# Channel attention and gated unit in seven-product blocks: the sums of GpSimd moved to VectorE and to accumulating DMAs, and two more of eight pairs in eight products

## The chip, the core and the metric

The kernel runs on one core of one Trainium2 chip. The core has five engines that run side by side, each through its own queue in order: TensorE (PE, with PEld for its weight loads), VectorE (DVE), ScalarE (ACT), GpSimd (POOL) and SyncE (SP, which here only issues DMAs). The metric is the device time of one execution in microseconds.

## The reference, cut to what matters

```python
qn = q / (norm(q, axis=1) + 1e-6);  kn = k / (norm(k, axis=1) + 1e-6)    # over the 6080 tokens
s  = kn.transpose(0, 2, 1) @ qn / tau                                     # 4 batches of 256x256
a  = softmax(s, axis=-1);  y = v @ a                                      # y: 4 x 6080 x 256
h  = y.reshape(24320, 256) @ w_in                                         # 256 -> 2048
out = (h * sigmoid(1.702 * h)) @ w_out                                    # 2048 -> 256
```

All inputs are float32; the two weights come as float64 and are narrowed on the chip.

## The kernel before, in words

**Work.** For each batch the scores are summed over 25 units of up to two rows of 128 tokens (`Attention.unit`), and beside them the sums of squares of q and k for the norms. The softmax gives `a`, and `weights` folds it into the first weight, so that h is v times one matrix. The 6080 tokens of a batch are cut into six chunks of 1024 (the last of 960). The 2048 features are cut into eight pairs of blocks of 2x128. So the main loop has 4 x 6 x 8 = 192 places, one pair at a place; `front` makes h and its gates for it, `back` the share of the output.

**Products.** A product is three matmuls of 128x128 by 128x512, since each float32 operand is split into a high and a low part in float32r (a cast on ScalarE makes the high part, a subtraction on VectorE, `low`, the other). `front` makes the four blocks of h in seven products (M1 to M7) of sums of blocks of v (`values`) and of the weights. `back` does the second multiplication, by G, the gated blocks, in one of two ways. In a pair of the first kind ("S") it forms four sums of gated blocks, P1 to P4, and makes seven products; in a pair of the second kind ("N") it needs no sums and makes eight. `GROUPS` says how many pairs of each kind stand in each half of a chunk: three S and one N. The first chunk of batch 0 has N pairs alone.

**Buffers.** Tiles live in named slots, and the next tile in a slot waits for every user of the one before. Sums of an S pair: `gp` (one slot) and, in place, `ga` (two). Split parts: `gi` and `gj` (two each), `gr` (three, `NR`). Second weights: `wo` (two). At the end of each half chunk one PSUM bank, K, is used four times in a row: it is read out as `ka`, `kb`, `kc` and `kd`; the last takes the products of N pairs, whose `gj` and `wo` are held until then.

**Who sums.** P1, P2 and P4 are made by VectorE, P3 by GpSimd (line 868). The four sums of v of a chunk are GpSimd's (`eng="POOL"`, line 705). The squares of batch 0 are added half by VectorE, half by GpSimd; those of batches 1 to 3 by GpSimd alone (lines 489 to 499). Batches 0 and 1 load q and k four rows at a time into the slots `gr` and `gj`, before the main loop needs these; for batch 1 the squares go through the slot `gp`, one tile at a time, and run beside the first chunk.

**Order.** The program is not written in its final order. Each instruction is a node with an engine, an estimated cost, dependencies and a due time; `Plan.order` plays the engines against each other, gives a free engine the ready node with the earliest due time, and the resulting sequence is issued. A load's landing is estimated as 50 ns + 2.6 ns per KB, plus a `lag` (line 261). Once issued, each engine keeps its sequence: an instruction that waits holds all behind it on its engine.

Of the kernel before, what the change touches and what calls it, by code (L numbers as in the profile page):

```python
# [11 lines left out]
F32 = mybir.dt.float32  # L12
F32R = mybir.dt.float32r
U32 = mybir.dt.uint32
AF = mybir.ActivationFunctionType
ALU = mybir.AluOpType
# [4 lines left out]
P = 128  # L21
# [4 lines left out]
HW = CH // 2  # L26
# [153 lines left out]
    return 350 + 2.0 * n  # L180


GROUPS = ((3, 1), (3, 1))
FIRST = ((0, 4), (0, 4))
NV = 8
NR = 3
GLAG = 12.0


# [1 line left out]
def channel_attention_then_glu(  # L191
# [10 lines left out]
    nc = tc.nc  # L202
# [9 lines left out]
    RT = 4  # L212
# [8 lines left out]
    g = Plan()  # L221

    def sbuf(slot, shape, dtype=F32, name=None):
        return g.buf(slot, lambda: sb.tile(list(shape), dtype, tag=slot, name=name or slot))
# [31 lines left out]
    def plain(ap):  # L256
        return ap.bitcast(F32) if ap.dtype == F32R else ap

    def load(dst, src, kb, deps=(), uses=(), due=0.0):
        return g.add(  # L260
            "SP", 50 + kb * 2.6, lambda: nc.sync.dma_start(plain(dst()), plain(src())), deps, uses, due, lag=2200,
        )

    def load_cast(dst, src, kb, deps=(), uses=(), due=0.0):
# [156 lines left out]
    class Attention:  # L421
# [39 lines left out]
        def unit(self, u, due, after=()):  # L461
            t0, nt, pp = self.units[u]
            if t0 not in self.raw:
                t = sbuf(f"ra{u % 2}", [P, 2, UT, C], F32, "raw")
                view = (lambda i: t()[:, i, :nt, :]) if pp == P else (lambda i: t()[:pp, i, 0, :])
                ns = [
                    load(
                        lambda i=i: view(i), lambda i=i: self.rows(i, t0, nt, pp), 128 * nt, after, [t], due - 8,
                    )
                    for i in range(2)  # L470
                ]
                for o in range(nt):
                    self.raw[t0 + o] = (t, o, ns)
            buf, o, _ = self.raw[t0]
            ready = [n for j in range(nt) for n in self.raw[t0 + j][2]]
            w = 2 * nt * C
            src = lambda: buf()[:pp, :, o : o + nt, :]
            acc = self.acc
            if u == 0:
                self.acc_n = [g.add(  # L480
                    "ACT", act(w), lambda: nc.scalar.activation(acc(), src(), AF.Square), ready, [buf, acc], due + 0.5,
                )]
            else:
                sq = sbuf("gp" if self.b == 1 else "sq", [P, 2, UT, C], F32, "sq")
                s = g.add(
                    "ACT", act(w),
                    lambda: nc.scalar.activation(sq()[:pp, :, :nt, :], src(), AF.Square), ready, [buf, sq], due + 1,  # L487
                )
                if self.b == 0:
                    parts = [("DVE", slice(0, 1)), ("POOL", slice(1, 2))]  # L490
                else:
                    parts = [("POOL", slice(0, 2))]
                new = []
                for e, (eng, sl) in enumerate(parts):
                    a = lambda sl=sl: acc()[:pp, sl, :nt, :]
                    new.append(tt(
                        a, a, lambda sl=sl: sq()[:pp, sl, :nt, :], ALU.add, w // len(parts),
                        [s, self.acc_n[min(e, len(self.acc_n) - 1)]], [sq, acc], due + 1.5, eng,
                    ))
                self.acc_n = new  # L500
            if self.direct:
                op, ok, uses = buf, ready, [buf]
            else:
                hl = sbuf("hl", [P, 2, UT, 2, C], F32R, "hl")
                hs = [
                    load_cast(
                        lambda i=i: hl()[:, i, :nt, 0, :] if pp == P else hl()[:pp, i, 0, 0, :],
                        lambda i=i: self.rows(i, t0, nt, pp), 128 * nt, after, [hl], due - 6,
                    )
                    for i in range(2)  # L510
                ]
                l = low(
                    lambda: hl()[:pp, :, :nt, 1, :], src, lambda: hl()[:pp, :, :nt, 0, :], w,
                    hs + ready, [buf, hl], due,
                )
                ok, uses = [l], [hl]
            S = self.S if self.direct else bank("Z", "s")
            news = []
            for j in range(nt):
                first = j == 0 and (u == 0 or not self.direct)  # L520

                def fn(j=j, first=first):
                    for i in range(NC2):
                        ci = slice(i * P, (i + 1) * P)
                        out = S()[:, i * C : (i + 1) * C]
                        begin = first and i == 0
                        if self.direct:
                            nc.tensor.matmul(
                                out, lhsT=buf()[:pp, 1, o + j, ci], rhs=buf()[:pp, 0, o + j, :],
                                start=begin, stop=True, skip_group_check=True,  # L530
                            )
                            continue
                        for m, (l, r) in enumerate(((0, 0), (0, 1), (1, 0))):
                            nc.tensor.matmul(
                                out, lhsT=hl()[:pp, 1, j, l, ci], rhs=hl()[:pp, 0, j, r, :],
                                start=begin and m == 0, stop=True, skip_group_check=True,
                            )

                n = g.add(
                    "PE", 864 if self.direct else 720, fn, ok + [self.first] + news[:1], [*uses, S], due + 2 + 0.1 * j,  # L540
                )
                if first and self.direct:
                    self.first = n
                news.append(n)
            if self.direct:
                self.last += news
            else:
                total = self.S
                self.last = [
                    g.add("DVE", dve(HW), lambda: nc.vector.tensor_copy(total(), S()), news, [S, total], due + 2.5)  # L550
                    if u == 0 else
                    tt(
                        lambda: total(), lambda: S(), lambda: total(), ALU.add, HW, news + self.last, [S, total],
                        due + 2.5,
                    )
                ]
# [145 lines left out]
    vslot = [0]  # L702
    ORDER = (M1, M2, M6, M5, M7, M3, M4)

    def values(b, c, due, after=(), eng="POOL"):
        o, w = chunks[c]
        hw = w // 2
        raw = sbuf("vr", [P, NC2, CH], F32, "v_raw")
# [107 lines left out]
    def back(ck, u, fr, wo, wb, t):  # L816
# [50 lines left out]
                    product(acc, a(i), src, j, ok, at)  # L867
                at += 0.7
        else:
            gp = sbuf("gp", [P, 2, HW], F32, "gp")  # L870
            gr = sbuf(f"gr{rcount[0] % NR}", [P, 2, 2, HW], F32R, "gr")
            rcount[0] += 1
            p1 = tt(lambda: gp()[:, 0, :hw], blk(0), blk(1), ALU.add, hw, [g11, g12], [ga, gp], t + 8.2)
            p3 = tt(blk(0), blk(0), blk(3), ALU.add, hw, [p1, g22], [ga], t + 8.8, "POOL")
            p2 = tt(lambda: gp()[:, 1, :hw], lambda: gp()[:, 0, :hw], blk(3), ALU.add, hw, [p1, g22], [ga, gp], t + 9.4)
            p4 = tt(blk(2), blk(2), lambda: gp()[:, 1, :hw], ALU.add, hw, [p2, g21, lo], [ga, gp], t + 12)
            hr = cast(lambda: gr()[:, 0, :, :hw], lambda: gp()[:, :, :hw], 2 * hw, [p1, p2], [gp, gr], t + 15)
            lr = low(
                lambda: gr()[:, 1, :, :hw], lambda: gp()[:, :, :hw], lambda: gr()[:, 0, :, :hw], 2 * hw,
                [hr], [gp, gr], t + 16,  # L880
            )
            pair = lambda: ga()[:, 0:3:2, :hw]
            hj = cast(lambda: gj()[:, 0, :, :hw], pair, 2 * hw, [p3, p4], [ga, gj], t + 13)
            lj = low(
                lambda: gj()[:, 1, :, :hw], pair, lambda: gj()[:, 0, :, :hw], 2 * hw, [hj], [ga, gj], t + 14,
            )
            a = lambda i: (lambda m: wt()[:, m, i, :])
            ck.k1.append(product(K, a(M1), gi, 0, lo, t + 13))
# [90 lines left out]

    def fetch_wo(ck, u, due, after=()):  # L980
        woslot[0] += 1
        w = sbuf(f"wo{woslot[0] % 2}", [P, 2, NI, P], F32R, "wo")
        cut = slice(1, 1 + NI) if ck.kinds[u][2] else slice(0, 4)
        n = load(
            lambda: w()[:, :, : cut.stop - cut.start], lambda: wout_d[u, :, :, cut, :], 640,
            [wout_ready[u], *after], [w], due,
        )
        return w, n
# [18 lines left out]
    keep_warm(8, (), -9e8, "X")  # L1007
    EARLY = -400.0
    t0, slot = 0, 0
    stage = ["gr0", "gj0", "gr1", "gj1", "gr2"]  # L1010
    sizes = [UT] + [RT] * ((T + 1 - UT + RT - 1) // RT)
    tau_n = None
    for r, room in enumerate(sizes):
# [21 lines left out]
    nxt = Attention(1)  # L1035
    t0, slot = 0, 0
    while t0 < T:
        nxt.load_direct(t0, RT, f"gr{slot % 3}", -80.0 + 2.2 * t0)
        t0 += RT
        slot += 1  # L1040
    for u in range(nu):
# [96 lines left out]
```

## Time and profile before

| | |
|---|---|
| median of 3 runs | 2467.65 us (2467.39 to 2470.84) |
| profiled execution | 2472.11 us, of it 2470.3 us from first to last instruction |
| PE busy | 2207.9 us (89%) |
| DVE busy | 1943.2 us (79%) |
| ACT busy | 1647.6 us (67%) |
| POOL busy | 700.1 us (28%) |
| mean granted TensorE clock | 0.971 of full |

An engine's busy time counts its instructions from start to end, with whatever slows them down; idle time is told by what ended it. Of PE, a busy stretch is not a stretch at full rate: matmuls overlap, and the clock that was granted has two levels.

### The profile page before, as it was taken

How to read it: one execution, taken by the hardware profiler on the slowest of the kernel's cores; microseconds unless marked ns; L12 is line 12 of the kernel's file. 1: busy time of each engine (PE TensorE's matmuls, PEld its weight loads, DVE VectorE, ACT ScalarE, POOL GpSimd, SP SyncE). 2: the span in 40 equal slices, each digit the busy share in tenths (PEclk: the TensorE clock that was granted, in tenths of full speed). 3: DMA queues.
4: the chain of work that ended last, by engine and by line, in shares of the span. 5: the costliest groups of instructions: out<-in, count | busy, mean ns of one | idle time of the engine just before them, and what ended most of it. 6: DMA issues, size and time to landing. Idle time of an engine off the chain costs nothing.

```text
span 2470.3 us, 27428 instructions
## 1 busy us (share of the span) xinstructions
PE 2207.9 (89%) x9694; PEld 1762.4 (71%) x9694; DVE 1943.2 (79%) x2167; ACT 1647.6 (67%) x2355; POOL 700.1 (28%) x440
## 2 busy tenths in 40 slices
PE   8588899989988899989898899989999999999998
PEld 7466677767776677767677677767777777777777
DVE  5888877778778787877887877878787777877776
ACT  4466776766656667766576666767777777777775
POOL 4442212334333331213333343322122122212211
PEclk9699999999999999999999999999999999999999
DMA  8676666566565654866566656656765555545553
GB/s 283 209 257 245 235 255 233 186 221 226 190 222 184 226 179 159 285 236 202 194 212 218 223 176 212 204 188 224 253 215 194 179 192 196 192 159 202 190 181 137
DMA packets 206872, 517.19 MB, mean 209 GB/s; under 512 B 16272, under 2 KB 84880, under 8 KB 205712
## 3 DMA queue, kind: packets, MB, share of 16 engines
q1 hardware_dynamic: 180816, 490.53, 56.6%
q0 software_dynamic: 25920, 24.91, 4.3%
q8 instruction: 77, 1.26, 0.2%
q14 instruction: 59, 0.48, 0.1%
HBM read 448.53 MB, written 66.85 MB: 209 GB/s over the span
## 4 chain that ended last, share of the span: by engine, by line
PE 42%; DVE 26%; DMA 16%; ACT 8%; issue 4%; POOL 3%; SPq 0%; DVEq 0%; POOLq 0%; ACTq 0%
PE ps_o L764 11%; PE ps_k L764 8%; PE ps_X L764 8%; PE ps_Y L764 6%; PE ps_Z L764 5%; DMA wo<-wout_d 5%; DVE ga L276 4%; DVE gi L291 3%; DMA hl<-in_k 3%; DVE gp L276 3%; ACT ga L790 3%; DMA raw<-in_k 3%; DVE gj L291 2%; DVE hl L291 2%; DVE v L291 2%
## 5 line engine op out<-in xcount | busy, mean ns | idle before, releaser
L275 POOL TENSOR_TENSOR ga<-ga 128x512 f32<-128x512 f32 (+1 forms) x138 | 229.6, 1664 | 1044.0 <-DVE gp L276 1016.2
L764 PE MATMUL ps_X<-v,w 128*128 128x512 f32 (+1 forms) x1728 | 498.2, 397 | 17.0 <-ACT ps_Z L268 16.6
L790 ACT ACTIVATE ga<-ga 128x512 f32<-128x512 f32 (+1 forms) x384 | 235.6, 626 | 258.1 <-DVE ga L276 256.6
L764 PE MATMUL ps_o<-gi,wo 128*128 128x512 f32 (+1 forms) x1476 | 401.3, 394 | 1.9 <-DVE gi L291 1.3
L291 DVE TENSOR_TENSOR gi<-ga,gi 128x1536 fp32r<-128x1536 f32 (+2 forms) x192 | 344.7, 1796 | 68.2 <-ACT gi L268 67.9
L764 PEld LDWEIGHTS ps_X<-v,w 128*128 128x128 f32 x1728 | 322.4, 191 | 99.8 <-ACT ps_Z L268 37.7
L764 PE MATMUL ps_Y<-v,w 128*128 128x512 f32 (+1 forms) x1152 | 337.9, 402 | 45.5 <-DVE ga L276 37.0
L764 PE MATMUL ps_Z<-v,w 128*128 128x512 f32 (+1 forms) x1152 | 333.3, 397 | 27.4 <-DVE ss L276 12.4
L764 PE MATMUL ps_o<-gj,wo 128*128 128x512 f32 (+1 forms) x1152 | 316.6, 396 | 28.6 <-DVE oc L276 8.0
L275 POOL TENSOR_TENSOR acc<-acc,sq 128x1024 f32<-128x1024 f32 (+2 forms) x96 | 216.6, 2257 | 389.9 <-ACT sq L487 389.8
L764 PEld LDWEIGHTS ps_o<-gi,wo 128*128 128x128 f32 x1476 | 281.5, 191 | 61.8 <-DVE gi L291 2.8
L764 PEld LDWEIGHTS ps_Y<-v,w 128*128 128x128 f32 x1152 | 212.8, 192 | 111.2 <-DVE ga L276 53.3
L764 PEld LDWEIGHTS ps_Z<-v,w 128*128 128x128 f32 x1152 | 216.5, 191 | 86.8 <-DVE ss L276 18.8
L764 PEld LDWEIGHTS ps_o<-gj,wo 128*128 128x128 f32 x1152 | 214.9, 190 | 83.5 <-DVE gj L291 11.0
L268 ACT CAST gi<-ga 128x1536 fp32r<-128x1536 f32 (+2 forms) x192 | 258.5, 1346 | 5.1
L276 DVE TENSOR_TENSOR ga<-ps_Y,m 128x512 f32<-128x512 f32 (+1 forms) x192 | 130.4, 679 | 153.0 <-PE ps_Y L764 96.7
L764 PE MATMUL ps_k<-gr,wb 128*128 128x512 f32 (+1 forms) x828 | 217.4, 390 | 3.4 <-ACT kb L268 1.3
L291 DVE TENSOR_TENSOR gj<-ga,gj 128x1024 fp32r<-128x1024 f32 (+1 forms) x138 | 192.6, 1396 | 21.6 <-ACT gj L268 20.3
L268 ACT CAST gj<-ga 128x1024 fp32r<-128x1024 f32 (+1 forms) x138 | 143.9, 1043 | 76.4 <-DVE ga L276 70.1
L764 PE MATMUL ps_k<-gi,wo 128*128 128x512 f32 (+1 forms) x414 | 133.0, 424 | 69.0 <-DMA wo<-wout_d 45.7
L291 DVE TENSOR_TENSOR gr<-gp,gr 128x1024 fp32r<-128x1024 f32 (+1 forms) x138 | 185.0, 1340 | 5.6 <-ACT gr L268 5.4
L268 ACT CAST gr<-gp 128x1024 fp32r<-128x1024 f32 (+1 forms) x138 | 143.5, 1040 | 58.5 <-DVE gp L276 47.7
(120 smaller groups left out, 3269.7 us busy)
## 6 DMA issues: line engine op xcount, KB each, us to landing
w<-w_d SPq DMA_DIRECT2D x184, 896.0 KB, 4.7
wo<-wout_d SPq DMA_DIRECT2D x138, 640.0 KB, 5.5
wb<-wout_d SPq DMA_DIRECT2D x138, 256.0 KB, 3.8
wo<-wout_d SPq DMA_DIRECT2D x54, 512.0 KB, 4.9
w_d<-wst SPq DMA_DIRECT2D x24, 896.0 KB, 5.1
v_raw<-in_vT SPq DMA_DIRECT2D x20, 1024.0 KB, 8.8
out_T<-oc SPq DMA_DIRECT2D x80, 256.0 KB, 5.4
wi<-win_d SPq DMA_DIRECT2D x32, 512.0 KB, 5.6
```

The costliest lines, as they stand in the source:

```text
L268: return g.add("ACT", act(n, psum), lambda: nc.scalar.copy(dst(), src()), deps, uses, due)
L275: return g.add("POOL", pool(n), lambda: nc.gpsimd.tensor_tensor(dst(), a(), b(), op=op), deps, uses, due)
L276: return g.add("DVE", dve(n), lambda: nc.vector.tensor_tensor(dst(), a(), b(), op=op), deps, uses, due)
L291: lambda: nc.vector.tensor_tensor(dst(), src(), hi().bitcast(F32), op=ALU.subtract),
L764: nc.tensor.matmul(dst, lhsT=l(a), rhs=r(b), start=begin and n == 0, stop=True, skip_group_check=True,)
L790: lambda: nc.scalar.activation(dst(), src(), AF.Gelu_apprx_sigmoid, scale=sign), deps, uses, at,
```

## The change

1. **GROUPS**: two S and two N pairs in each half of a chunk in place of three and one. With the first chunk as it was, 92 of the 192 places are S pairs and 100 are N pairs (138 and 54 before).
2. **P1 and P3** of an S pair are one VectorE operation of 2x512 elements, which reads one block twice (`broadcast_to`). P1 to P4 all stand in `gp`, now four blocks; nothing is written into `ga` any more.
3. **The sums of v** are VectorE's.
4. **The squares of batches 1 to 3** are added by DMAs that accumulate into `acc`, issued by GpSimd. Batch 0 is as it was.
5. **Slots and estimates**: two slots of `gr` in place of three, three of `wo` in place of two; the loads of batches 0 and 1 go through one `gr` slot less; a load's lag is 3000 ns in place of 2200.

```diff
-GROUPS = ((3, 1), (3, 1))
+GROUPS = ((2, 2), (2, 2))
-NR = 3
+NR = 2
+NWO = 3
@@ load
-... deps, uses, due, lag=2200,
+... deps, uses, due, lag=3000,
@@ Attention.unit
-                if self.b == 0:
-                    parts = [("DVE", slice(0, 1)), ("POOL", slice(1, 2))]
-                else:
-                    parts = [("POOL", slice(0, 2))]
+                parts = [("DVE", slice(0, 1)), ("POOL", slice(1, 2))] if self.b == 0 else [("DMA", slice(0, 2))]
...
+                    if eng == "DMA":
+                        new.append(g.add(
+                            "POOL", 1200, lambda a=a, more=more: nc.gpsimd.dma_start(a(), more(), accum_op=ALU.add),
+                            deps, [sq, acc], due + 1.5, lag=3500,
+                        ))
@@ values
-    def values(b, c, due, after=(), eng="POOL"):
+    def values(b, c, due, after=(), eng="DVE"):
@@ back, a pair of the first kind
-            gp = sbuf("gp", [P, 2, HW], F32, "gp")
+            gp = sbuf("gp", [P, 4, HW], F32, "gp")
-            p1 = tt(lambda: gp()[:, 0, :hw], blk(0), blk(1), ALU.add, hw, [g11, g12], [ga, gp], t + 8.2)
-            p3 = tt(blk(0), blk(0), blk(3), ALU.add, hw, [p1, g22], [ga], t + 8.8, "POOL")
-            p2 = tt(lambda: gp()[:, 1, :hw], lambda: gp()[:, 0, :hw], blk(3), ALU.add, hw, [p1, g22], [ga, gp], t + 9.4)
-            p4 = tt(blk(2), blk(2), lambda: gp()[:, 1, :hw], ALU.add, hw, [p2, g21, lo], [ga, gp], t + 12)
+            p13 = tt(
+                lambda: gp()[:, 0:3:2, :hw], lambda: ga()[:, 0:1, :hw].broadcast_to([P, 2, hw]),
+                lambda: ga()[:, 1:4:2, :hw], ALU.add, 2 * hw, [g11, g12, g22], [ga, gp], t + 8.2,
+            )
+            p2 = tt(lambda: gp()[:, 1, :hw], lambda: gp()[:, 0, :hw], blk(3), ALU.add, hw, [p13], [ga, gp], t + 9.4)
+            p4 = tt(lambda: gp()[:, 3, :hw], blk(2), lambda: gp()[:, 1, :hw], ALU.add, hw, [p2, g21], [ga, gp], t + 12)
...
@@ fetch_wo, loads of batches 0 and 1
-        w = sbuf(f"wo{woslot[0] % 2}", [P, 2, NI, P], F32R, "wo")
+        w = sbuf(f"wo{woslot[0] % NWO}", [P, 2, NI, P], F32R, "wo")
-    stage = ["gr0", "gj0", "gr1", "gj1", "gr2"]
+    stage = ["gr0", "gj0", "gr1", "gj1"]
-        nxt.load_direct(t0, RT, f"gr{slot % 3}", -80.0 + 2.2 * t0)
+        nxt.load_direct(t0, RT, f"gr{slot % 2}", -80.0 + 2.2 * t0)
```

In the orders below the numbers tell tiles of one name apart. VectorE at one S pair of the last batch, before: P1, P2 and P4, and the low parts of `gr` and `gj` (P3 is GpSimd's).

```order
L276 TENSOR_TENSOR gp_12905<-ga_12832 128x512
L276 TENSOR_TENSOR gp_12905<-gp_12905,ga_12832 128x512
L276 TENSOR_TENSOR ga_12832<-ga_12832,gp_12905 128x512
L291 TENSOR_TENSOR gr_12924<-gp_12905,gr_12924 128x1024
L291 TENSOR_TENSOR gj_12931<-ga_12832,gj_12931 128x1024
```

The same place now:

```order
L277 TENSOR_TENSOR gp_14672<-ga_14646 128x2x512
L277 TENSOR_TENSOR gp_14672<-gp_14672,ga_14646 128x512
L277 TENSOR_TENSOR gp_14672<-ga_14646,gp_14672 128x512
L292 TENSOR_TENSOR gi_14677<-ga_14646,gi_14677 128x1536
L292 TENSOR_TENSOR gr_14697<-gp_14672,gr_14697 128x1024
```

The first operation is twice as wide and no operation of GpSimd stands between it and `gj`.

GpSimd in the last batch before, with the sums of v (`v_t`, `v_raw`) between the P3 of six pairs:

```order
L275 TENSOR_TENSOR v_t_14793<-v_raw_14744 128x512
L275 TENSOR_TENSOR ga_14736<-ga_14736 128x512
L275 TENSOR_TENSOR v_t_14793<-v_t_14793,v_raw_14744 128x512
L275 TENSOR_TENSOR v_raw_14744<-v_raw_14744 128x512
L275 TENSOR_TENSOR ga_14913<-ga_14913 128x512
```

VectorE at such a place now:

```order
L277 TENSOR_TENSOR ga_15117<-ps_X_15063,m5_15089 128x512
L277 TENSOR_TENSOR v_t_15150<-v_raw_15099 128x512
L277 TENSOR_TENSOR v_t_15150<-v_t_15150,v_raw_15099 128x512
L277 TENSOR_TENSOR v_raw_15099<-v_raw_15099 128x512
L283 SCALAR_TENSOR_TENSOR gj_15157<-ga_15117,gj_15157 128x1024
L292 TENSOR_TENSOR gi_15174<-ga_15117,gi_15174 128x1024
```

Three of the four sums of v stand in VectorE's queue behind the load of `v_raw` and ahead of a pair's low parts; GpSimd's queue has no sums there any more.

ScalarE in the first chunk before, at the end of batch 1's squares (`sq`), in front of the sixth pair (`m5` begins a pair):

```order
L487 ACTIVATE sq_1295<-raw4_1063 128x2x256
L268 COPY m5_1314<-ps_Z_1305 128x512
L268 CAST cw_1320<-cv_1271 128x512
L268 COPY ps_Z_1305<-ps_X_1310 128x512
L487 ACTIVATE sq_1330<-raw4_1063 64x2x256
L268 COPY ps_Y_1344<-ps_X_1310 128x512
```

The same squares now, one or two pairs further on:

```order
L269 COPY m5_1495<-ps_Z_1485 128x512
L269 COPY ps_Z_1485<-ps_X_1490 128x512
L269 CAST cs_1502<-cf_1466 128x1024
L269 COPY ps_Y_1512<-ps_X_1490 128x512
L488 ACTIVATE sq_1515<-raw4_1359 128x2x256
L793 ACTIVATE ga_1520<-ps_Z_1485 128x512
L793 ACTIVATE ga_1520<-ga_1520 128x512 x2
L852 ACTIVATE gj_1547<-ga_1520 128x1024
L269 COPY wf_1549<-ps_w_1527 128x512
L793 ACTIVATE ga_1520<-ps_Y_1512 128x512
L269 CAST gi_1555<-ga_1520 128x1024
L488 ACTIVATE sq_1562<-raw4_1359 64x2x256
```

The last square of batch 1 now stands in the seventh pair of the first chunk. Each square waits until the DMA that adds the one before it has landed, and what stands behind it on ScalarE waits with it.

## Rows read from the trace of the kernel before

**Rows 1.** The page: engines, and the granted TensorE clock in 40 slices.
```profile
PE 2207.9 (89%) x9694; PEld 1762.4 (71%) x9694; DVE 1943.2 (79%) x2167; ACT 1647.6 (67%) x2355; POOL 700.1 (28%) x440
PEclk9699999999999999999999999999999999999999
```
**Rows 2.** Stages: us, PE, PEld, DVE, ACT, POOL busy, clock, DMA share, GB/s.
```profile
0.00:266.00 266.00, 207.33 (x904) 169.23 (x905) 209.08 (x261) 142.91 (x194) 108.61 (x64) 0.91 0.71 245
266.00:1864.00 1598.00, 1435.27 (x6369) 1143.03 (x6368) 1275.09 (x1400) 1079.11 (x1547) 475.80 (x311) 0.97 0.63 213
1864.00:2471.00 607.00, 565.29 (x2424) 450.18 (x2422) 459.07 (x506) 425.61 (x617) 115.71 (x66) 0.99 0.53 183
```
**Rows 3.** Waits of PE: us in total, times, longest us.
```profile
PE ps_k L764 <- DMA wo<-wout_d: 45.7, 32, 5.3
PE ps_Y L764 <- DVE ga L276: 37.0, 29, 5.4
...
PE ps_k L764 <- DVE gi L291: 22.0, 17, 3.9
...
PE ps_s L534 <- DVE hl L291: 15.9, 19, 2.9
PE ps_Z L764 <- DVE ss L276: 12.4, 10, 3.5
```
**Rows 4.** Timeline near 1210 us: start, us, instruction, idle time before it.
```profile
1210.56 2.36 POOL L275 TENSOR_TENSOR acc<-acc,sq 128x1024 f32<-128x1024 f32 x1 [6.16 <-ACT sq L487]
1210.63 2.83 DVE L276 TENSOR_TENSOR ga<-ga,gp 128x512 f32<-128x512 f32 x1
...
1214.12 0.97 PE L764 MATMUL ps_Y<-v,w 128*128 128x512 f32 x3 [2.37 <-DVE ga L276]
```
**Rows 5.** VectorE by line and shape: count, busy us, mean ns, idle before.
```profile
L291 DVE TENSOR_TENSOR gi<-ga,gi 128x1536 fp32r<-128x1536 f32 x114 | 234.2, 2054 | 47.3 <-ACT gi L268 47.1
...
L291 DVE TENSOR_TENSOR gr<-gp,gr 128x1024 fp32r<-128x1024 f32 x114 | 154.1, 1352 | 5.2 <-ACT gr L268 5.1
...
L276 DVE TENSOR_TENSOR ga<-ga,gp 128x512 f32<-128x512 f32 x114 | 100.3, 880 | 3.4
```
**Rows 6.** Instructions on tile gp, on VectorE: ns min/median/max, first and last start.
```profile
L276 DVE TENSOR_TENSOR gp<-ga x138: 641/692/2760, 273.5 to 2443.6; 128x512 f32<-128x512 f32 x114, 128x480 f32<-128x480 f32 x24
...
L276 DVE TENSOR_TENSOR ga<-ga,gp x138: 648/692/2830, 279.1 to 2449.1; 128x512 f32<-128x512 f32 x114, 128x480 f32<-128x480 f32 x24
L291 DVE TENSOR_TENSOR gr<-gp,gr x138: 1141/1218/3443, 286.3 to 2449.7; 128x1024 fp32r<-128x1024 f32 x114, 128x960 fp32r<-128x960 f32 x24
```
**Rows 7.** Instructions on tile gi, on VectorE.
```profile
L291 DVE TENSOR_TENSOR gi<-ga,gi x192: 1142/1752/2859, 144.6 to 2456.4; 128x1536 fp32r<-128x1536 f32 x114, 128x1024 fp32r<-128x1024 f32 x46, 128x1440 fp32r<-128x1440 f32 x24, 128x960 fp32r<-128x960 f32 x8
```
**Rows 8.** Chain of waits at 1249 us: start, us, one product.
```profile
1249.17 0.68 PE ps_X L764 x3
```
**Rows 9.** GpSimd by line and shape.
```profile
L275 POOL TENSOR_TENSOR acc<-acc,sq 128x1024 f32<-128x1024 f32 x66 | 170.8, 2588 | 307.8 <-ACT sq L487 307.7
...
L265 POOL DMA_DIRECT2D hl<-in_k x50 | 35.6, 712 | 0.0
```
**Rows 10.** Instructions on tile sq, from 79 to 240 us.
```profile
L275 POOL TENSOR_TENSOR acc<-acc,sq x28: 842/2386/3298, 77.9 to 225.6; 128x1024 f32<-128x1024 f32 x22, 128x512 f32<-128x512 f32 x3, 128x256 f32<-128x256 f32 x1, 64x256 f32<-64x256 f32 x1
L487 ACT ACTIVATE sq<-raw x27: 612/1054/1072, 80.1 to 224.9; 128x1024 f32<-128x1024 f32 x23, 128x512 f32<-128x512 f32 x2, 64x512 f32<-64x512 f32 x2
```
**Rows 11.** ScalarE's first copy of the eighth pair.
```profile
255.34 0.58 ACT L268 COPY m<-ps_Z 128x512 f32<-128x512 f32 x1
```
**Rows 12.** DMA issues: count, KB each, median us to landing.
```profile
v_raw<-in_vT SPq DMA_DIRECT2D x20, 1024.0 KB, 8.8
...
hl<-in_k POOLq DMA_DIRECT2D x46, 256.0 KB, 4.6
...
raw<-in_k SPq DMA_DIRECT2D x46, 256.0 KB, 5.5
...
raw<-in_k SPq DMA_DIRECT2D x21, 512.0 KB, 6.0
```

More of the change, by code (lines that the diff above doesn't have):

```diff
@@ L260, in load @@
         return g.add(
-            "SP", 50 + kb * 2.6, lambda: nc.sync.dma_start(plain(dst()), plain(src())), deps, uses, due, lag=2200,
+            "SP", 50 + kb * 2.6, lambda: nc.sync.dma_start(plain(dst()), plain(src())), deps, uses, due, lag=3000,
         )
@@ L495, in unit @@
                     a = lambda sl=sl: acc()[:pp, sl, :nt, :]
[L496 to L499, printed above, removed]
+                    more = lambda sl=sl: sq()[:pp, sl, :nt, :]
+                    deps = [s, self.acc_n[min(e, len(self.acc_n) - 1)]]
+                    if eng == "DMA":
[3 more added lines that the diff above has]
+                        ))
+                    else:
+                        new.append(tt(a, a, more, ALU.add, w // len(parts), deps, [sq, acc], due + 1.5, eng))
                 self.acc_n = new
@@ L869, in back @@
         else:
-            gp = sbuf("gp", [P, 2, HW], F32, "gp")
+            gp = sbuf("gp", [P, 4, HW], F32, "gp")
             gr = sbuf(f"gr{rcount[0] % NR}", [P, 2, 2, HW], F32R, "gr")
             rcount[0] += 1
-            p1 = tt(lambda: gp()[:, 0, :hw], blk(0), blk(1), ALU.add, hw, [g11, g12], [ga, gp], t + 8.2)
-            p3 = tt(blk(0), blk(0), blk(3), ALU.add, hw, [p1, g22], [ga], t + 8.8, "POOL")
-            p2 = tt(lambda: gp()[:, 1, :hw], lambda: gp()[:, 0, :hw], blk(3), ALU.add, hw, [p1, g22], [ga, gp], t + 9.4)
-            p4 = tt(blk(2), blk(2), lambda: gp()[:, 1, :hw], ALU.add, hw, [p2, g21, lo], [ga, gp], t + 12)
-            hr = cast(lambda: gr()[:, 0, :, :hw], lambda: gp()[:, :, :hw], 2 * hw, [p1, p2], [gp, gr], t + 15)
+            p13 = tt(
[4 more added lines that the diff above has]
+            p4 = tt(lambda: gp()[:, 3, :hw], blk(2), lambda: gp()[:, 1, :hw], ALU.add, hw, [p2, g21], [ga, gp], t + 12)
+            hr = cast(lambda: gr()[:, 0, :, :hw], lambda: gp()[:, :2, :hw], 2 * hw, [p13, p2], [gp, gr], t + 15)
             lr = low(
-                lambda: gr()[:, 1, :, :hw], lambda: gp()[:, :, :hw], lambda: gr()[:, 0, :, :hw], 2 * hw,
+                lambda: gr()[:, 1, :, :hw], lambda: gp()[:, :2, :hw], lambda: gr()[:, 0, :, :hw], 2 * hw,
                 [hr], [gp, gr], t + 16,
             )
-            pair = lambda: ga()[:, 0:3:2, :hw]
-            hj = cast(lambda: gj()[:, 0, :, :hw], pair, 2 * hw, [p3, p4], [ga, gj], t + 13)
+            hj = cast(lambda: gj()[:, 0, :, :hw], lambda: gp()[:, 2:, :hw], 2 * hw, [p13, p4], [gp, gj], t + 13)
             lj = low(
-                lambda: gj()[:, 1, :, :hw], pair, lambda: gj()[:, 0, :, :hw], 2 * hw, [hj], [ga, gj], t + 14,
+                lambda: gj()[:, 1, :, :hw], lambda: gp()[:, 2:, :hw], lambda: gj()[:, 0, :, :hw], 2 * hw,
+                [hj], [gp, gj], t + 14,
             )
```

## The prediction

> **What bounds the kernel now.** I read the page first: PE is busy 89% of the span and VectorE 79% [rows 1], so a further product can cost its full length, while VectorE should have room. Is PE's busy time work, though? In the chain of waits a product (three matmuls) takes 0.68 us where products follow each other [rows 8]. Next the stages. In the first 266 us (loads, batch 0's scores, first chunk) PE is idle for 59 us and the mean granted clock is 0.91 of full. From 266 to 1864 us (two more batches' scores beside the main loop) PE is idle for 163 us of 1598 and the clock is 0.97; from 1864 us on, the main loop alone, 42 us of 607 and 0.99 [rows 2]. VectorE's busy share goes the same way: 80% in the middle, 76% at the end. PE is held from outside, then, and most where VectorE has most to do. The clock is at the lower of its two levels (1.2 in place of 2.4 GHz) more often in the stages with more idle PE; after 266 us the missing share is worth 0.03 x 1598 + 0.01 x 607 = 54 us of work at full rate.
>
> PE's waits name the holders. After `wo` (45.7 us) come four waits for VectorE: `ga` 37.0, `gi` 22.0, `hl` 15.9 and `ss` 12.4, together 87.3 us [rows 3]. The timeline shows one at work. GpSimd adds squares for 2.36 us; VectorE's P4 starts 0.07 us later and takes 2.83 us, where its median is 0.69; PE then waits 2.37 us for a `ga` that was queued behind it [rows 4, 6]. VectorE's mean durations lie above the medians in every operation that reads two tiles from SBUF: `gi` 2.05 against 1.75 us, `gr` 1.35 against 1.22, P4 0.88 against 0.69 [rows 5 to 7]. Over 114 instructions of each that is 34 + 15 + 21 = 70 us in three of the groups alone. While GpSimd adds, VectorE stands still in part.
>
> **The change part by part.** All of it is summed against the profiled execution, 2472.1 us.
>
> Products: 92 places have S pairs in place of 138, so 46 pairs need one product more, 46 x 0.68 = **+31** us on PE [rows 8]. PE has no room of its own, so all of it counts.
>
> VectorE's load, by medians [rows 6, 7]: each of the 46 pairs loses three sums (3 x 0.69), the low part of `gr` (1.22) and a third of `gi`'s (1.75 to about 1.22), 3.82 us; 176 us in all. The 92 S pairs left get P1 and P3 in one operation of 1024 elements. No such sum is in the trace; a subtraction of that size takes 1.22 [rows 6], so 0.53 more than P1 alone, +49 us. 96 sums of v add 96 x 0.69 = 66 us. Net -61 us. With the 70 us of standing still or more, VectorE falls from 1943 to 1810 us or less. GpSimd keeps only batch 0's sums and DMA issues. ScalarE loses a cast of `gr` and a third of `gi`'s in 46 pairs, and is bound nowhere now.
>
> What does PE get of this? The four waits for VectorE are worth between 0 (they are latency and stay) and -87 (all go). I take two thirds, **-58**, since they sit in the stage where GpSimd's additions are densest (476 us of 1598, against 116 of 607 later [rows 2]). What is late next on those paths is ScalarE's gates and seeds.
>
> Wait for `wo`, 45.7 us: a load is issued just ahead of its use because the order assumes it lands sooner than it does. A third slot and 0.8 us more lag both help. The N pairs now hold two of three slots until the last use of bank K, so bounds are 0 and -45.7; I take three quarters, **-34**.
>
> v's sums in VectorE's queue: the first needs `v_raw`, which lands 8.8 us after issue [rows 12]; the order's estimate is 50 ns + 2.66 + 3.0 = 5.7 us. What is queued behind a late one is the next pair's `ga` and low parts, and PE behind those. 3.1 us x 23 chunks = 71 us if nothing hides it and all reaches PE; 0 if VectorE is behind its order anyway. I take a sixth, **+12**: VectorE now has a quarter of its time free, and PE has other pairs' products to go on with.
>
> Clock: less idle PE, fewer falls. Bounds 0 and -54; I take the share in which I let PE's waits go, somewhat under half, **-24**.
>
> Accumulating DMAs, batch 1. Here the change adds a wait. Squares go through one tile `sq`, so the next square starts only when the last has landed in `acc`. Before, the chain is square 1.05 us, GpSimd's sum 2.39, and it ran for 24 sums from about 80 to 228 us, 6.2 us each, mostly waiting for other work [rows 10]; the eighth pair begins at 255.3 [rows 11]. Now a step is the square 1.05, the issue on GpSimd 0.71 [rows 9], hand-overs of some 0.1, and the landing. No accumulating DMA is in the trace. Its bounds by the nearest rows: 4.6 us (a DMA from GpSimd with half the bytes) and 8.8 us (a load with twice the bytes, as if the destination counted as well); the nearest in size is `raw`, 512 KB, 6.0 us [rows 12]. I take 6.0: a step of 7.9 and 24 steps, the last two of half the size or less, some 185 us from 80 on, so 265 us. In the new order the last square stands inside the seventh pair, where before 255 us were reached: **+10** us. With 4.6 (6.5 us a step, end near 235) nothing is lost; with 8.8 (10.7 us, end near 335) some +80. GpSimd's queue holds only the chain there; ScalarE's and, through the slots of raw rows, SP's hold the first chunk's casts and weight loads behind it. The 48 DMAs of batches 2 and 3 are a pair or more apart and have time to land. One `gr` slot less for the loads of batches 0 and 1 I cost at nothing: four slots of 1 MB remain, and a load of half a slot lands within 6 us. `gj` and K: an S pair's `gj` now waits for bank K's last use one pair earlier than before; GLAG puts the products that need it some pairs later, so nothing.
>
> The page SBUF — State Buffer of the Trainium skill (section SBUF: two separate sides) has a rule against this part: a DMA issued from GpSimd needs its descriptors written by GpSimd, and a VectorE operation in a two-port fast mode locks it out meanwhile. Here loads from GpSimd land no later than SyncE's of the same 256 KB (4.6 against 5.5 us), and VectorE's low parts take 1.2 ns per element, not half of that [rows 6, 12]; by the rule the sum would become that of the slow chain below, by the rows it stays.
>
> The page DMA: Bandwidth & Descriptors (section Anatomy of one DMA — SWDGE (gpsimd) path) fits 2.0 us plus bytes by 436 GB/s, for 512 KB an estimate of 3.2 us and a chain that ends near 202 us: then the +10 would be 0. The trace's 4.6 us for half the bytes is already above it.
>
> Sum: 31 - 58 - 34 + 12 - 24 + 10 = -63, so 2409 for an execution like the profiled one. That one took 4.5 us more than the median of the runs shown (2467.65), so the forecast is **2405 us**.
>
> **The rivals.**
>
> *More comes free.* GpSimd's additions cost VectorE more than the three groups show: 138 P3, 96 sums of v and 72 of squares go, and every VectorE operation behind a held one is late too. For it: rows 4; against it: waits for ScalarE remain. If all four waits and the wait for `wo` go, two thirds of the clock's loss, and the chain hides: 31 - 87 - 46 + 12 - 36 = -126, **2342**.
>
> *The waits are latency.* If PE's waits are set by the chain of casts, gates and subtractions rather than by VectorE's load, they stay: 31 - 34 + 12 + 10 = +19 less a quarter of the four waits (22), **2465**. For it: in the last stage GpSimd adds little and PE is still idle for 7% [rows 2].
>
> *v's sums hold VectorE.* All 71 us reach PE: 2405 + 59 = **2464**.
>
> *The slow chain,* the one on the other side. From a landing of 8.5 us on, the squares of batch 1 set the pace of the first chunk, as above; ScalarE stands at a square while gates behind it are ready, and the eighth pair begins past 330 us. Without the chain the sum is -73; 80 + 24 steps - 255 makes that up from a step of 10.3 us on, a landing of 8.5. At a landing of 11 the step is 12.9, the end 389, the loss 134: 2467.65 - 73 + 134 = **2528**. For it: reads of source and destination in one DMA, next to a queue that is 71% busy there [rows 2]; against it: 512 KB loads take 6.0 under the same load.
>
> **How the numbers follow.** Forecast (2370 to 2440): 0.50. More comes free: 0.17. Waits are latency: 0.11. v's sums: 0.08. Slow chain: 0.14. A difference within 0.2% (4.9 us) can't be told from none here. Faster by more: 0.50, 0.17, and 0.10 of the middle two, 0.77. Within: 0.05, of the middle two. Slower: the slow chain and 0.04 of the middle two, 0.18. The range leaves out the lower third of "more comes free" and the upper half of the slow chain: 2340 to 2495.
>
> **What would show it.** Right: `gr`, `gi` and P4 on VectorE at means near their medians; VectorE under 1820 us busy; PE's waits for `ga`, `gi`, `hl` and `ss` near 30 us and for `wo` near 12; the clock at 0.98 from 266 us on; the last square of batch 1 at about 265 us and first copy of the eighth pair near 265. Wrong: ScalarE's waits for a DMA at `sq` of over 60 us in the first chunk (slow chain); VectorE's waits for `v_raw` near 70 us; PE's waits for VectorE unchanged though its durations fell (latency).

## The result, and the profile after

The changed kernel takes 2346.11 us (median of 3 runs, 2342.52 to 2349.61) against 2467.65: a ratio of 0.9504, 95% interval 0.9478 to 0.9529. The forecast was 2405; the gain is 122 us where 63 were expected. Below, times of different runs are compared by their ratios to the kernel before, which was measured beside each run on the same chip; 0.001 is 2.5 us.

The page of the changed kernel, engines and granted clock; it answers to [rows 1].

```profile
PE 2184.9 (93%) x9832; PEld 1789.5 (76%) x9832; DVE 1650.3 (70%) x2079; ACT 1583.5 (68%) x2309; POOL 179.3 (8%) x206
...
PEclk9798899999999999999999999999999999999999
```

PE does 138 matmuls more in 23 us less busy time: part of its busy time before was not work at full rate (the rows do not say how much of it was the lower clock). VectorE loses 293 us, more than the 61 us of work and the 70 us of standing still that the prediction could name.

The stages, to be set beside [rows 2] (us, PE, PEld, VectorE, ScalarE, GpSimd busy, clock, DMA share, GB/s):

```profile
0.00:266.00 266.00, 194.27 (x814) 154.03 (x814) 148.35 (x230) 119.72 (x160) 57.01 (x52) 0.89 0.84 256
266.00:1864.00 1598.00, 1518.83 (x6939) 1246.50 (x6940) 1159.41 (x1451) 1120.63 (x1645) 122.32 (x155) 0.98 0.73 237
1864.00:2345.00 481.00, 471.82 (x2081) 388.94 (x2079) 342.56 (x399) 343.13 (x507) 0.00 (x0) 1.00 0.53 184
```

After 266 us PE is idle for 88 us in place of 204. In the first stage it does 814 matmuls where it did 904: the start got slower.

PE's waits, against [rows 3]:

```profile
PE ps_Y L767 <- ACT ps_Y L269: 22.5, 9, 5.4
...
PE ps_s L537 <- DVE hl L292: 7.9, 11, 1.3
...
PE ps_Y L767 <- DVE ga L277: 3.0, 5, 1.0
...
PE ps_k L767 <- DMA wo<-wout_d: 0.4, 1, 0.4
PE ps_k L767 <- DVE gi L292: 0.2, 1, 0.2
```

The four waits for VectorE fell from 87.3 to 11.1 us (`ss` no longer shows), that for `wo` from 45.7 to 0.4.

VectorE by shape, against [rows 5]: the means are now the medians of [rows 6, 7].

```profile
L292 DVE TENSOR_TENSOR gi<-ga,gi 128x1536 fp32r<-128x1536 f32 x76 | 133.3, 1754 | 33.1 <-ACT gi L269 32.4
...
L277 DVE TENSOR_TENSOR gp<-ga 128x1024 f32<-128x1024 f32 x76 | 92.9, 1222 | 21.1 <-ACT ga L793 20.2
...
L292 DVE TENSOR_TENSOR gr<-gp,gr 128x1024 fp32r<-128x1024 f32 x76 | 92.6, 1219 | 6.6 <-ACT gr L269 6.6
...
L277 DVE TENSOR_TENSOR gp<-ga,gp 128x512 f32<-128x512 f32 x76 | 52.4, 689 | 3.4
```

P1 and P3 in one operation take 1.22 us, as was assumed from the subtraction of that size.

The DMAs, against [rows 12]. An accumulating DMA lands in 5.9 us at the median; `hl`, in the same queue of GpSimd, now needs 6.8 in place of 4.6.

```profile
acc<-sq POOLq DMA_DIRECT2D x66, 512.0 KB, 5.9
...
hl<-in_k POOLq DMA_DIRECT2D x46, 256.0 KB, 6.8
```

And the chain of batch 1, two of its 24 steps in the timeline, with the eighth pair's first copy against [rows 11]:

```profile
187.22 0.86 POOL L498 DMA_DIRECT2D acc<-sq  x1 [10.29 <-ACT sq L488]
193.50 1.06 ACT L488 ACTIVATE sq<-raw 128x1024 f32<-128x1024 f32 x1 [1.16 <-DMA acc<-sq]
194.85 0.86 POOL L498 DMA_DIRECT2D acc<-sq  x1 [6.77 <-ACT sq L488]
204.10 1.06 ACT L488 ACTIVATE sq<-raw 128x1024 f32<-128x1024 f32 x1 [4.80 <-DMA acc<-sq]
205.45 0.86 POOL L498 DMA_DIRECT2D acc<-sq  x1 [9.74 <-ACT sq L488]
...
290.86 0.98 POOL L498 DMA_DIRECT2D acc<-sq  x1 [5.77 <-ACT sq L488]
294.01 0.58 ACT L269 COPY m<-ps_Z 128x512 f32<-128x512 f32 x1
```

The steps shown are 7.6 and 10.6 us, the last sum of the chain is issued only at 291 us, and the eighth pair begins at 294, 39 us later than before.

### The profile page after: what moved, and what is told of

Read it like the earlier page. It is cut to its first block, busy times and chain, and to the rows that moved or that the text cites. A ratio compares the mean times of both kernels' runs of the same rounds, so it can differ in the third digit from the quotient of the medians.

```text
span 2344.4 us, 27182 instructions
## 1 busy us (share of the span) xinstructions
PE 2184.9 (93%) x9832; PEld 1789.5 (76%) x9832; DVE 1650.3 (70%) x2079; ACT 1583.5 (68%) x2309; POOL 179.3 (8%) x206
## 4 chain that ended last, share of the span: by engine, by line
PE 63%; DMA 20%; DVE 7%; ACT 6%; issue 2%; POOL 1%; SPq 1%; DVEq 0%; ACTq 0%
PE ps_o L767 21%; PE ps_X L767 12%; PE ps_k L767 9%; PE ps_Y L767 9%; PE ps_Z L767 8%; DMA acc<-sq 5%; DMA hl<-in_k 4%; DMA raw<-in_k 4%; PE ps_s L537 2%; DMA out_T<-oc 2%; ACT ga L793 2%; PE ps_w L684 2%; ACT sq L488 1%; DMA wi<-win_d 1%; DMA v_raw<-in_vT 1%
## 5 line engine op out<-in xcount | busy, mean ns | idle before, releaser
L767 PE MATMUL ps_o<-gi,wo 128*128 128x512 f32 (+1 forms) x1752 | 460.1, 389 | 1.7 <-DVE gi L292 1.7
L292 DVE TENSOR_TENSOR gi<-ga,gi 128x1536 fp32r<-128x1536 f32 (+2 forms) x192 | 280.6, 1462 | 49.3 <-ACT gi L269 48.4
L488 ACT ACTIVATE sq<-raw 128x1024 f32<-128x1024 f32 (+1 forms) x96 | 98.2, 1023 | 181.7 <-DMA acc<-sq 73.5
L269 ACT COPY ps_Y<-ps_X 128x512 f32<-128x512 f32 (+1 forms) x192 | 109.3, 570 | 120.4 <-PE ps_X L767 119.2
L283 DVE SCALAR_TENSOR_TENSOR gj<-ga,gj 128x1024 fp32r<-128x1024 f32 (+1 forms) x100 | 121.2, 1212 | 76.4 <-ACT gj L852 76.0
L767 PE MATMUL ps_k<-gj,wo 128*128 128x512 f32 (+1 forms) x600 | 155.6, 390 | 2.6 <-DVE kc L277 1.8
L767 PE MATMUL ps_k<-gr,wb 128*128 128x512 f32 (+1 forms) x552 | 145.9, 388 | 0.0
L269 ACT COPY m<-ps_Z 128x512 f32<-128x512 f32 (+1 forms) x192 | 110.4, 575 | 39.1 <-PE ps_Z L767 39.0
L277 DVE TENSOR_TENSOR ga<-ps_X,m 128x512 f32<-128x512 f32 (+1 forms) x192 | 130.7, 681 | 5.6 <-PE ps_X L767 5.5
L793 ACT ACTIVATE ga<-ps_Y 128x512 f32<-128x512 f32 (+1 forms) x192 | 112.6, 587 | 30.3 <-PE ps_Y L767 29.4
```

The costliest lines, as they stand in the source:

```text
L269: return g.add("ACT", act(n, psum), lambda: nc.scalar.copy(dst(), src()), deps, uses, due)
L277: return g.add("DVE", dve(n), lambda: nc.vector.tensor_tensor(dst(), a(), b(), op=op), deps, uses, due)
L283: lambda: nc.vector.scalar_tensor_tensor(dst(), in0=a(), scalar=-1.0, in1=b(), op0=ALU.mult, op1=ALU.subtract,),
L292: lambda: nc.vector.tensor_tensor(dst(), src(), hi().bitcast(F32), op=ALU.subtract),
L767: nc.tensor.matmul(dst, lhsT=l(a), rhs=r(b), start=begin and n == 0, stop=True, skip_group_check=True,)
L793: lambda: nc.scalar.activation(dst(), src(), AF.Gelu_apprx_sigmoid, scale=sign), deps, uses, at,
```

## The experiments

At first the theory was the prediction's: GpSimd's sums were what held the kernel. The rival was that VectorE's work as such, or the order, did. Since the order is computed, an edit changes it too, and what a new order brings or costs is part of each difference below.

**Batch 1's squares on VectorE.**

```diff
-... if self.b == 0 else [("DMA", slice(0, 2))]
+... if self.b == 0 else [("DVE" if self.b == 1 else "DMA", slice(0, 2))]
```

> The changed kernel, but batch 1's squares are added by VectorE (1.22 us each, 24 of them) and not by accumulating DMAs; batches 2 and 3 as changed. Theory (the chain of accumulating DMAs sets the pace of the first chunk, 190 us there against 140 before): the second chunk begins at 250 to 270 us in place of 306, and the time falls to 2295 to 2315 us. Rival (the first chunk is held by the weight conversions and their loads, which only stand beside the chain): it still begins near 300 us, time 2335 to 2350.

Measured: 2286.96 us, ratio 0.9264 (0.9242 to 0.9286), 59 us under the changed kernel. The second chunk begins at 247 us in place of 306; both lie just under the ranges of the theory. The first copy of the second chunk, in the changed kernel and in this run:

```profile
306.16 0.58 ACT L269 COPY m<-ps_Z 128x512 f32<-128x512 f32 x1
...
247.31 0.58 ACT L269 COPY m<-ps_Z 128x512 f32<-128x512 f32 x1
```

The chain of accumulating DMAs sets the first chunk's pace. That cost is a choice of the change, not a need: VectorE had the time. In the kernel before, with these sums on GpSimd, the second chunk began at 266 us, so against that kernel the chain costs 40 us there, and against VectorE 59.

**GpSimd busy for nothing.**

```diff
+            for i in range(2):
+                idle_n[0] = tt(
+                    lambda: idle, lambda: idle, lambda: idle, ALU.mult, HW, [*here, idle_n[0]], (), t + 4 + 4 * i, "POOL",
+                )
```

> The changed kernel, and at each of the 192 places GpSimd does two multiplications of 128x512 on a tile that nothing else uses, 384 of them, about as much GpSimd time (some 640 us) as its sums took before. Nothing waits for them but GpSimd's own DMA issues. Theory (VectorE stands still while GpSimd reads and writes SBUF, and that was what PE waited for): VectorE's busy time goes up by 150 us or more at the same instructions, PE's waits for VectorE come back to 50 us or more, time 2400 to 2470. Rival (the gain came from less VectorE work and a better order): VectorE may get longer, but the time stays within 20 us of 2346.

Measured: 2447.89 us, ratio 0.9909 (0.9877 to 0.9941), so 100 us slower than without by the ratios. The 384 operations wait for little but GpSimd's queue, and the last began at 1877 us. Engines, GpSimd's group, `gi` on VectorE, and PE's two longest waits for VectorE in the main loop:

```profile
PE 2221.6 (91%) x9832; PEld 1797.1 (73%) x9832; DVE 1867.2 (76%) x2080; ACT 1583.2 (65%) x2309; POOL 745.1 (30%) x590
```
```profile
L277 POOL TENSOR_TENSOR idle<-idle 128x512 f32<-128x512 f32 x384 | 578.9, 1508 | 22.7
```
```profile
L293 DVE TENSOR_TENSOR gi<-ga,gi 128x1536 fp32r<-128x1536 f32 x76 | 148.8, 1957 | 28.3 <-ACT gi L270 28.2
```
```profile
PE ps_Y L769 <- DVE ga L278: 24.5, 23, 4.1
...
PE ps_o L769 <- DVE gj L284: 21.2, 20, 3.7
```

With one memset more, VectorE is busy for 217 us longer, and `gi` is back near the 2.05 us of [rows 5]. PE's waits for VectorE's `ga`, `gj`, `hl` and `gi` come to 80 us in place of 18. GpSimd's work alone, with data that nobody needs, holds VectorE and costs about 100 us. A rival that was not set down is that these operations delay GpSimd's own DMA issues. The trace speaks against it: PE does the same 814 matmuls in the first 266 us, the second chunk begins at 304.5 us, and VectorE's wait for `hl` is 45.6 us in place of 66.4. The order is no rival either: some 96% of VectorE's and of ScalarE's instructions stand in the same order as in the changed kernel. The theory holds so far.

**Three S pairs again, sums off GpSimd.**

```diff
-GROUPS = ((2, 2), (2, 2))
-NR = 2
-NWO = 3
+GROUPS = ((3, 1), (3, 1))
+NR = 3
+NWO = 2
```

> The changed kernel with three S and one N pair in each half chunk as before, three gr slots and two wo slots (small tiles are packed closer to make room). All sums stay off GpSimd. Theory (GpSimd's sums were the loss): the gain stays, PE has 31 us less work, VectorE some 125 us more; 2315 to 2355. Rival (the gain came from two of eight pairs giving up their sums and low parts): most of it is lost, 2400 or more. If the third wo slot matters, PE's waits for wo come back to over 20 us.

Measured: 2422.72 us, ratio 0.9819 (0.9802 to 0.9837): 77 us are lost, as the rival had it. The expectation was wrong, and so was the theory as the whole of it. PE's longest wait is for `wo` again:

```profile
PE ps_k L767 <- DMA wo<-wout_d: 33.8, 29, 4.0
```

**The kernel before with two S and two N pairs,** two `wo` slots.

```diff
-GROUPS = ((3, 1), (3, 1))
+GROUPS = ((2, 2), (2, 2))
```

> The kernel before with one edit: two S and two N pairs in each half chunk. GpSimd keeps its sums. Theory (GpSimd's sums were the loss): GpSimd's sums fall only by 46 P3 (77 us of some 630), PE gets 31 us more; VectorE falls by some 180 us; time 2425 to 2475. Rival (VectorE's load as such, whatever slows it): 2360 to 2400.

Measured: 2448.93 us, ratio 0.9933 (0.9909 to 0.9956), as the theory had it; but this could not tell the sums from the slot.

**Two `wo` slots in the changed kernel** (`NWO = 2`).

> The changed kernel with two wo slots in place of three. With three S pairs, two wo slots and no sums on GpSimd the kernel was 77 us slower than the changed one. Theory A (the third wo slot makes most of that): PE's waits for wo come back to 30 us or more, time 2385 to 2425. Theory B (VectorE's and ScalarE's work in S pairs makes it: 46 pairs more with three sums and a low part of gr): time 2340 to 2365, waits for wo under 15 us.

Measured: 2406.30 us, ratio 0.9748 (0.9725 to 0.9771), 60 us slower, as theory A had it. PE's waits for `wo` are 32.9 us at bank K and 13.5 us at the other banks. The 60 us would be most of the 77 of the run with three S pairs, if the slot is worth as much there; that was not tried.

**The lag.** In the changed kernel back at 2200 ns, and in the kernel before at 3000 ns (one number each).

> The changed kernel with the estimated lag of a load at 2200 ns as before; only the order changes. If the lag is part of the gain (loads' users placed too early stand in their engine's queue): PE's waits for DMAs and VectorE's for raw and v_raw grow, time 2355 to 2375. If not: within 8 us of 2346.

> The kernel before with a load's lag at 3000 ns; only the order changes. If the lag alone took PE's waits for wo (45.7 us before) away: 2425 to 2450, waits for wo under 20 us. If GpSimd's sums hold the kernel anyway: 2455 to 2475.

Measured: 2352.58 us, ratio 0.9534 (0.9508 to 0.9560), whose interval overlaps that of the changed kernel (0.9478 to 0.9529), so no effect shown; and 2437.73, ratio 0.9871 (0.9848 to 0.9894), 32 us faster. That time is in the range of "the lag alone", but 26.2 us of waits for `wo` at bank K are left where under 20 were expected. A reading that fits, and was not tested apart: the lag helps where loads are issued just ahead of their use, and does little where a slot more lets them go early. Either run differs by nothing but the order, so a new order alone can be worth 32 us.

**The kernel before with two and two pairs, three `wo` slots and two `gr` slots;** and, as its control, with two `gr` slots alone.

```diff
-GROUPS = ((3, 1), (3, 1))
+GROUPS = ((2, 2), (2, 2))
...
-NR = 3
+NR = 2
...
-        w = sbuf(f"wo{woslot[0] % 2}", [P, 2, NI, P], F32R, "wo")
+        w = sbuf(f"wo{woslot[0] % 3}", [P, 2, NI, P], F32R, "wo")
... (the loads of batches 0 and 1 go through one `gr` slot less)
```

> The kernel before with two S and two N pairs in each half chunk, three wo slots and two gr slots, as the changed kernel has; GpSimd keeps all its sums, the lag stays 2200 ns. With two wo slots and three gr slots it was 2449 us, and the changed kernel was 60 us faster with three wo slots than with two. Theory A (the wo slot and GpSimd's sums are two losses side by side): some 60 us less, 2380 to 2400, waits of PE for wo under 10 us. Theory B (behind GpSimd's sums the slot is worth little): 2425 to 2450.

> The kernel before with two S and two N pairs in each half chunk and two gr slots in place of three (one less for the loads of batches 0 and 1 too), two wo slots, all sums on GpSimd. Against this, the run at 2358 us has a third wo slot and nothing else. Theory (the third wo slot made the 91 us): 2440 to 2460, as with three gr slots (2449). Rival (the gr slots, or the other loads of the start, did): 2400 or less.

Measured: 2357.66 us, ratio 0.9546 (0.9516 to 0.9576), with the slot; 2461.88 us, ratio 0.9972 (0.9944 to 0.9999), without. The slot is worth some 105 us, more than either theory gave it, with all of GpSimd's sums in place. The trace of the run with two pairs each, two `wo` slots and three `gr` slots (2448.93 us) shows how the slot comes in (its timeline at the end of a half chunk):

```profile
2117.73 3.01 PE L764 MATMUL ps_k<-gj,wo 128*128 128x512 f32 x12
...
2119.41 1.88 SPq L261 DMA_DIRECT2D wo<-wout_d  x2
...
2123.41 0.98 PE L764 MATMUL ps_Z<-v,w 128*128 128x512 f32 x3 [2.67 <-ACT ga L790]
...
2125.32 1.62 PE L764 MATMUL ps_k<-gi,wo 128*128 128x512 f32 x3 [0.93 <-DMA wo<-wout_d]
```

Both N pairs hold their `wo` until bank K's last products. Only from 2119.4 us on are the next two loads issued, and until the first has landed PE does no product of the second multiplication; in between it does one product of the next pair's first multiplication, which waits for a gate. Of 3.6 us of idle time here the rows put 2.67 down to that gate and 0.93 to `wo`. Over the whole run more of it has the right name. PE's waits for `wo`, at bank K and at the other banks (`ps_o`), without the third slot and with it:

```profile
PE ps_k L764 <- DMA wo<-wout_d: 49.5, 28, 5.7
...
PE ps_o L764 <- DMA wo<-wout_d: 9.1, 9, 2.2
```
```profile
PE ps_k L764 <- DMA wo<-wout_d: 4.9, 3, 2.5
...
PE ps_o L764 <- DMA wo<-wout_d: 1.3, 1, 1.3
```

The two profiled executions are 87 us apart. PE's idle time falls by 64 us, 52 of them under the name of `wo`, and its busy time by 24 us (2211.8 to 2188.2) with the same matmuls; the granted clock is 0.971 in the one and 0.976 in the other, which is an estimate of 11 of these 24 us (2212 x 0.005). So the waits named `wo`, 59 us, are about half of the 105 us. This edit also makes a new order (some 69% of VectorE's and 54% of ScalarE's instructions stand as without the slot), and how much of the 105 us that is was not told apart.

**Less on GpSimd still.** The changed kernel with the squares of batches 0 and 1 on VectorE alone, and with those of all four (the edit of the second; in the first, batches 2 and 3 keep `DMA`).

```diff
-parts = [("DVE", slice(0, 1)), ("POOL", slice(1, 2))] if self.b == 0 else [("DMA", slice(0, 2))]
+parts = [("DVE", slice(0, 2))]
```

> The changed kernel with the squares of batches 0 and 1 added by VectorE alone, so that GpSimd adds nothing. Against the run with batch 1's squares on VectorE (2287 us): in batch 0 a step of the chain was square 1.06, then GpSimd's half 1.3 to 1.8 beside VectorE's half that was drawn out to 1.75 at times, 2.9 to 3.3 us a step; now 1.06 + 1.22 + hand-overs, 2.4 us. If that chain sets the start: 12 to 20 us less, 2267 to 2277. If the loads of q and k do: within 5 us of 2287.

> The changed kernel with the squares of all four batches added by VectorE: no accumulating DMA and no sum on GpSimd is left. Against the run with those of batches 0 and 1 on VectorE (2275 us): VectorE gets 48 sums of 1.22 us more (59 us of some 670 us that it is idle); the loads of hl, which share GpSimd's queue with the accumulating DMAs and land in 6.4 to 6.8 us with them and 4.2 to 4.6 before, come sooner. If the queue counts: 2255 to 2270, VectorE's wait for hl's DMA (66 us in the changed kernel) under 30. If VectorE's time counts: 2278 to 2300.

Measured: 2275.24 us, ratio 0.9211 (0.9186 to 0.9237), and 2255.82, ratio 0.9134 (0.9109 to 0.9159). Both times are as the first of their two outcomes had it, but the sign that was to go with the second is missing: VectorE's wait for `hl`'s DMA is 48.7 us, where under 30 was expected, and `hl` still lands in 6.1 us at the median. The last is the best version found, 4% under the changed kernel. Its engines:

```profile
PE 2157.9 (96%) x9832; PEld 1771.4 (79%) x9832; DVE 1715.5 (76%) x2151; ACT 1587.0 (70%) x2309; POOL 76.0 (3%) x110
```

VectorE works 65 us more than in the changed kernel, and PE has less idle time all the same. Both groups of accumulating DMAs, batch 1's and those of batches 2 and 3, cost more time than sums on VectorE.

## Why the prediction was right or wrong, point by point

The path from the kernel before to the changed one can be walked in runs (ratios times 2467.65): two and two pairs with two `gr` slots, -7 us; the third `wo` slot, -105; the lag, and all sums from GpSimd to VectorE with P1 and P3 in one operation, -102 (to the run at 2256); then back the way the change has them: batches 2 and 3 squared by DMAs +19, half of batch 0 on GpSimd +13, batch 1 by DMAs +59. Together -122, but for rounding. Another sequence of the same steps would share it out otherwise: the slot taken out of the changed kernel is worth 60, not 105.

- *Direction and range* hold: 2346 us lies in 2340 to 2495. The size was half of what came, by terms that missed in both directions.
- *Products, +31.* Consistent with the traces: the last stage runs with PE busy for 472 of 481 us, so products count in full. The run with two and two pairs alone shows them only in a net of -17, with VectorE's and ScalarE's lighter load against them.
- *The wait for `wo`, -34, was sized worst.* It took 45.7 us as an end of the range, since that is the sum of waits with that name at bank K. It saw that the N pairs would hold two of three slots, and took that for a reason to gain less; it did not price what two N pairs do when there are only two. In the runs two N pairs without a third slot gain next to nothing (-7 and -17), though VectorE is busy for 237 us less in the second, and the slot is worth 105 us with GpSimd's sums and 60 without. The groups and the slot together bring -112; the prediction's terms for products, `wo`, VectorE and the clock come to -85 in all. Waits named `wo` are half of the 105; the rest stood under other names and in PE's busy time. What a third slot is worth with three S pairs and one N wasn't tried.
- *VectorE standing still, -58, and the clock, -24.* The mechanism is shown: idle work on GpSimd brings it back, +217 us on VectorE and +100 us in time. The size was under: -102 with all sums on VectorE, of which the lag is a few. From the run at 2358 to that at 2256 VectorE takes over all of GpSimd's sums, and its busy time stays the same (1716.6 and 1715.5 us). The 70 us counted from three groups were 217 in the run with idle work. The clock came as forecast: 0.98 and 1.00 after 266 us, which by the prediction's own reckoning is 22 us. The rival that more comes free was right about VectorE. That its sum, 2342, is so near to 2346 is luck: it has the chain of DMAs hidden and the wait for `wo` at -46.
- *v's sums, +12.* VectorE's wait for `v_raw` is 15.3 us in 14 times, far from 71, and no wait of PE leads there. Their own cost wasn't measured apart.
- *The accumulating DMAs, +10: the right place and mechanism, the size was off by 29.* The eighth pair begins 39 us later than before and not 10; against sums on VectorE the chain costs 59. The landing was taken as 6.0 us and is 5.9 at the median over the run, but in this chain, with DMA engines busy for 84% of the first 266 us (71% before), landings take 4.5 to 11.1 us, 6.4 at the median; from the first issue at 90.6 to the landing at 295 us the 24 steps average 8.5 where 7.9 were assumed. The chain also began 10 us later than assumed. The sign that the prediction named for the slow chain came: ScalarE's squares wait 73.5 us for these DMAs in the first chunk, and over 60 was the sign. So the rival that ends on the other side took place in part, at 39 us of the 80 that its lower end gave, and was outweighed.
- *Batches 2 and 3, at nothing:* +19. Why is open. Their DMAs share a queue with `hl`, whose landing went from 4.6 to 6.8 us, and VectorE's wait for it rose from 20.5 to 66.4 us; the prediction did not count what is queued behind them. But without any accumulating DMA that wait is still 48.7 us, and in the run at 2358, which has none either, it is 84.8. ScalarE's squares wait 59.9 us for their rows of k in the run at 2275 and 28.7 in that at 2256, which may be another part.

Whether the Trainium skill's rule on descriptors that VectorE locks out (SBUF — State Buffer, section SBUF: two separate sides) had a part in the slow landings is not shown: no run puts the chain beside more or less VectorE work. GpSimd's own part, the issue, took 0.85 to 1.22 us in all 24 steps.

## What to carry to other kernels

The sum of the waits under one name is not what their cause costs. Here 59 us under the name of `wo` were worth about 105, since an engine goes on with what is left and part of its idle time appears under the names of that work. Ask for each slot how many holders the new order has at once before pricing it. And a running sum through DMAs is a chain of full landings: one that is hidden in the main loop can set the pace in a stretch where the same steps come every few microseconds.

## What the runs showed of the hardware

GpSimd's elementwise operations draw out VectorE's that read SBUF alone, whatever the data: 579 us of idle multiplications made VectorE 217 us longer. VectorE's additions that read one operand from PSUM escape. In the trace of the kernel before, of VectorE's 128x512 float32 operations, 182 that read SBUF alone ran beside a sum of GpSimd and took 1.07 us on average, up to 2.83; the 219 others took 0.70 at most. Of 545 with an operand from PSUM 131 ran beside one, and none took more than 0.70. One group of these, 192 of them:

```profile
L276 DVE TENSOR_TENSOR ga<-ps_Y,m x192: 641/683/693, 133.6 to 2452.0; 128x512 f32<-128x512 f32 x160, 128x480 f32<-128x480 f32 x32
```
